# A sparse-attention kernel: early loads moved into five groups that wait for GpSimd

## The chip, the cores and the metric

The kernel runs on one core of a Trainium2 chip. The core has TensorE (PE, matmuls, with PEld for its weight loads), VectorE (DVE), ScalarE (ACT), GpSimd (POOL) and SyncE (SP, which here only issues DMAs). All DMAs of the core run on the same 16 DMA engines. The metric is device time in microseconds (us) of one execution; lower is better. On three runs the kernel before took 883.36, 886.07 and 886.86 us.

## The reference

```python
def _attn_ref(q, k, v):                      # q, k, v: 4 x 8 x 576 x 64
    scores = scale * np.matmul(q, k.transpose(0, 1, 3, 2))
    # heads 0-3: mask_local, the last 32 positions; heads 4-7: mask_strided, every 32nd
    scores = np.where(masks[None], scores, -1000000000.0)
    scores = scores - np.max(scores, axis=-1, keepdims=True)
    attn = np.exp(scores)
    attn = attn / (np.sum(attn, axis=-1, keepdims=True) + 1e-09)
    return np.matmul(attn, v)

def reference(...):
    x = attn_out as 2304 tokens x 512
    x = (sigmoid(x @ w_gate) * (x @ w_val)) @ w_out        # 512 -> 1536 -> 512
    return softplus(x @ w_in) @ w_out2                     # 512 -> 2048 -> 512
```

All of it is in fp32; a weight reaches the chip as 64-bit words, which the kernel takes apart into a high and a low part.

## The kernel before

The program is written in a fixed order by hand; nothing reorders it, so each engine works through its own instructions in the order of the code. Attention comes first. It is cut into 16 **units**, numbered 0 to 15: one batch and one pair of heads each, and in every four units two local and two strided ones. A unit i goes through these steps: `bias` and `scores` (PE matmuls into `ps_s`; L1011, L1030), a maximum and a subtraction on DVE (L1048, L1049), `exponent` on ACT (L1056), `normalize` (a sum and a reciprocal on DVE, L1063 to L1066, and the multiplication on POOL, L1069, in two halves), `p_transposes` (PE, L1090, copied out by ACT), `values` (PE, L1107) and `outputs`. `first()` runs units 0 to 3 and the start of unit 4 (`TURN`) with little else to fill PE; `stage(u)` then runs units 5 on, with the matmuls of the first dense layer (`ps_g`, `ps_v`, `ps_y`) between its steps. From about 220 us on the program is dense layers alone.

**Loads.** SP issues one DMA after the other: `load(i)` brings q and k of unit i (L917, L918), `load_v(i)` its v in two DMAs (L931), and `load_next()` one **piece of words**, 128 x 512 words of 8 bytes (L104). q, k, v and the pieces have three buffers each. The pieces are taken apart ("decoded") by `decode_steps`: DVE reads the piece first at L122 and last at L139, then ACT and POOL write the weights; its argument `refill` says whether it asks for another piece at its end. In `first()` the pieces 0, 1 and 2 are decoded (`decs[0]` to `decs[2]`), in `stage(5)` piece 3. Because engines are in order, DVE's L122 for piece 3 stands between unit 5's L1049 and L1063, and a late piece 3 holds up unit 5.

SP can have eight DMAs under way: each one uses one of eight semaphores in turn and waits for the DMA that had it before.

Of the kernel before, what the change touches and what calls it, by code (L numbers as in the profile page):

```python
# [9 lines left out]
F32 = mybir.dt.float32  # L10
# [38 lines left out]
def tile_sparse_attention_moe_moe2(  # L49
# [10 lines left out]
    nc = tc.nc  # L60
# [35 lines left out]
    raws = {}  # L96
    queue, todo = [], []

    def load_next():
        if todo:  # L100
            g, m, c = piece = todo.pop(0)
            src = w1[g, m] if g < NG1 else w2[g - NG1, m // 2]
            raw = rawp.tile([P, PIECE], U64, tag="raw", name="raw")
            nc.sync.dma_start(out=raw, in_=src[:, c * PIECE:(c + 1) * PIECE])  # L104
            raws[piece] = raw
            queue.append(piece)
# [37 lines left out]
    def decode_steps(pools, refill=True):  # L144
        (g, m, c), low, high, f, e = fields(pools)
        hi, lo = (x[:, c * PIECE:(c + 1) * PIECE] for x in wset[g % 2][m])
        high_part(pools, high, f)
        yield
        ff, ef = f.bitcast(F32), e.bitcast(F32)
        nc.scalar.activation(out=hi, in_=ff, func=AF.Copy)  # L150
        low_part(pools, low, f, e)
        pools["e"].tensor_tensor(out=ff, in0=ff, in1=hi.bitcast(F32), op=ALU.subtract)
        nc.gpsimd.tensor_tensor(out=lo, in0=ff, in1=ef, op=ALU.add)  # L153
        if refill:
            load_next()
        yield
# [75 lines left out]
    held = []  # L232
# [635 lines left out]
    def attention():  # L868
        with ExitStack() as actx:
# [16 lines left out]
            pools = {  # L886
                "g": pool("gp", 1), "t": pool("tp", 2), "d": pool("decp", 1), "e": nc.gpsimd,
                "hy": pool("ps_hy", 3, space=PSUM), "x": pool("ps_x", 1, space=PSUM),
            }
# [18 lines left out]
            def start_of(loc, r, i):  # L908
                return (r * NL[0] + i) * LQ if loc else (r * RH + i * RG) * NJ

            def load(i):
                b, hp = units[i]
                loc, w, m, ns = dims(i)
                qn, kn = (S, S + STRIDE) if loc else (QPAD, QPAD - HP + SQ)
                qq = qp.tile([P, QPAD], F32, tag="q", name="qt")
                kk = kp.tile([P, QPAD], F32, tag="k", name="kt")
                nc.sync.dma_start(out=qq[:, 0:qn], in_=q[b, hp][:, 0:qn])  # L917
                (nc.scalar if i < 2 else nc.sync).dma_start(  # L918
                    out=kk[:, 0:kn], in_=k[b, hp][:, 0:kn]
                )  # L920
                qt[i], kt[i] = qq, kk

            def load_v(i):
                b, hp = units[i]
                loc, w, m, ns = dims(i)
                t = vp.tile([P, NL[0], 2, D], F32, tag="v", name="vt")
                src = vl[b, hp] if loc else vs[b, hp - NLP]
                for r in range(HR):
                    n = NL[r] if loc else NS
                    o = r * HP  # L930
                    nc.sync.dma_start(out=t[o:o + w, 0:n], in_=src[r * w:(r + 1) * w, 0:n])  # L931
                vt[i] = t
# [7 lines left out]
            load_v(0)  # L940
            load_next()
            load(2)
            load_v(1)

            scratch = acc[NBA - 1]
            ident = scratch[:, 0:P]
# [216 lines left out]

            def first():

                decs = [decode_steps(pools, refill) for refill in (False, True, True)]
                bias(0)
                scores(0)
                masks[False] = table("m_str", P + 2 * LK, SQ, SLOTS_S, strided)
                exponent(0)  # L1170
                keep_busy(1)
                normalize(0)
                bias(1)
                scores(1)
                load_v(2)
                load(3)
                load_next()
                next(decs[0])
                exponent(1)
                keep_busy(2)  # L1180
                p_transposes(0)
                normalize(1)
                next(decs[0])
                bias(2)
                scores(2)
                values(0)
                load(4)
                load_v(3)
                load_next()
                outputs(0)  # L1190
                exponent(2)
                normalize(2)
                p_transposes(1)
                bias(3)
                scores(3)
                values(1)
                load_v(4)
                load(5)
                load_next()
                outputs(1)  # L1200
                exponent(3)
                normalize(3)
                next(decs[1])
                keep_busy(1)
                p_transposes(2)
                values(2)
                load_v(5)
                load(6)
                outputs(2)
                p_transposes(3)  # L1210
                next(decs[1])
                values(TURN - 1)
                outputs(TURN - 1)
                bias(TURN)
                scores(TURN)
                exponent(TURN)
                normalize(TURN)
                next(decs[2])
                yield
                next(decs[2])  # L1220
                yield
# [95 lines left out]
            for u in range(START, NU + SKEW):  # L1317
                t, pos = divmod(u - START, NPAIR)
# [172 lines left out]
```

## Time and profile before

| | us |
|---|---|
| runs of the kernel before | 883.36, 886.07, 886.86 (median 886.07) |
| the profiled execution | 887.23 |
| its span, from first to last instruction | 885.4 |
| PE busy (matmul records) | 865.7 |
| DVE / POOL / ACT busy | 598.2 / 490.2 / 420.6 |

The profiled execution took 1.16 us more than the median. The span is read by stretches: a wait at the start counts in full if nothing later takes it up, since PE is the engine that ends the program. "issue" behind an idle time means that the engine waited for nothing that the profile shows. PEclk is the granted clock of PE, 1.00 for 2.4 GHz and 0.50 for 1.2 GHz.

### The profile page before, as it was taken

To read this page: it belongs to the slowest core of one execution; us is meant where nothing else is said; L and a number is where in the kernel's file an instruction comes from. 1 tells how busy PE (TensorE), PEld (TensorE's weight loads), DVE (VectorE), ACT (ScalarE), POOL (GpSimd) and SP (SyncE) were. 2 spreads that over 40 slices of the span, in tenths; PEclk is the share of its full clock that TensorE was granted. 3 is DMA by queue.
4 is the path that set the end of the run, shared out by engine and by line. 5 is a ranking of instruction groups with operands and counts; after the bars stand their busy time and mean duration, and the time that the engine had idled before them with its cause. 6 is when DMAs were issued, how large, how long until landed. Compare 5 with 4: busy or idle time off the path is not lost.

```text
span 885.4 us, 15378 instructions
## 1 busy us (share of the span) xinstructions
PE 865.7 (98%) x6010; PEld 725.0 (82%) x6010; DVE 598.2 (68%) x898; ACT 420.6 (48%) x680; POOL 490.2 (55%) x389
## 2 busy tenths in 40 slices
PE   7799999999999999999999999999999999999998
PEld 5578878888888888888888888888888878888887
DVE  6696776268878888878874645665756574656574
ACT  2366544423333333233333466666667575665641
POOL 5373321037888687788778625466536963343630
PEclk9699999999999999999999999999999999999999
DMA  9696460034675577566644245566575565545403
GB/s 276 179 247 163 122 161 4 1 105 134 241 257 191 190 254 233 180 214 231 223 164 165 72 145 181 192 198 196 195 233 183 192 219 183 187 148 182 151 1 118
DMA packets 61367, 153.01 MB, mean 173 GB/s; under 512 B 6160, under 2 KB 6672, under 8 KB 61296
## 3 DMA queue, kind: packets, MB, share of 16 engines
q1 hardware_dynamic: 61008, 151.42, 53.3%
q8 instruction: 47, 0.77, 0.4%
q10 hardware_dynamic: 288, 0.62, 0.2%
q14 instruction: 24, 0.20, 0.1%
HBM read 113.75 MB, written 38.27 MB: 172 GB/s over the span
## 4 chain that ended last, share of the span: by engine, by line
PE 68%; DVE 4%; ACT 3%; POOL 3%; issue 1%; DVEq 0%; POOLq 0%; ACTq 0%
PE ps_y L72 9%; PE ps_y L73 9%; PE ps_y L74 9%; PE ps_v L72 4%; PE ps_v L74 4%; PE ps_v L73 4%; PE ps_g L72 4%; PE ps_g L74 4%; PE ps_g L73 4%; PE ps_h L74 3%; PE ps_h L73 3%; PE ps_h L72 3%; PE ps_b L72 2%; PE ps_b L73 2%; PE ps_b L74 2%
## 5 line engine op out<-in xcount | busy, mean ns | idle before, releaser
L330 POOL TENSOR_TENSOR b<-b,b 128x512 f32<-128x512 f32 (+1 forms) x42 | 72.5, 1739 | 91.7 <-DVE gl L330 46.1
L241 ACT ACTIVATE gh<-ps_v 128x512 fp32r<-128x512 f32 (+1 forms) x60 | 33.3, 555 | 131.5 <-DVE ps_v L284 131.5
L304 DVE TENSOR_TENSOR acc<-ps_y,acc 128x512 f32<-128x512 f32 (+1 forms) x100 | 62.2, 634 | 48.0 <-PE ps_y L74 47.6
L333 ACT ACTIVATE gh<-b 128x1024 fp32r<-128x1024 f32 (+1 forms) x63 | 57.8, 917 | 40.7 <-DVE b L713 23.9
L469 DVE TENSOR_TENSOR acc<-ps_y,acc 128x512 f32<-128x512 f32 x66 | 44.8, 686 | 41.7 <-PE ps_y L74 40.7
L330 POOL TENSOR_TENSOR gl<-b,gh 128x1024 fp32r<-128x1024 f32 x20 | 49.2, 2458 | 36.5 <-ACT gh L333 36.5
L242 DVE TENSOR_TENSOR gl<-ps_v,gh 128x512 fp32r<-128x512 f32 (+1 forms) x60 | 38.3, 638 | 37.5 <-ACT gh L241 37.5
L189 POOL TENSOR_TENSOR a<-f,e 128x512 f32<-128x512 f32 x32 | 41.4, 1295 | 39.6 <-DVE e L139 39.6
L177 POOL TENSOR_TENSOR pair<-a,pair 128x512 fp32r<-128x512 f32 x32 | 41.5, 1298 | 31.7 <-ACT pair L176 31.7
L330 DVE TENSOR_TENSOR gl<-b,gh 128x1024 fp32r<-128x1024 f32 (+1 forms) x43 | 48.7, 1134 | 14.5 <-ACT gh L333 14.3
L74 PE MATMUL ps_y<-gh,w02l 128*128 128x512 f32 (+1 forms) x144 | 53.8, 374 | 0.4 <-POOL w02l L153 0.4
L72 PE MATMUL ps_y<-gh,w12h 128*128 128x512 f32 (+1 forms) x144 | 54.1, 376 | 0.1
L73 PE MATMUL ps_y<-gl,w12h 128*128 128x512 f32 (+1 forms) x144 | 53.7, 373 | 0.0
L126 DVE SCALAR_TENSOR_TENSOR f<-raw,ps_x 128x512 uint32<-128x512 uint32 x68 | 46.8, 688 | 9.4 <-POOL w11l L153 2.1
L284 DVE TENSOR_TENSOR ps_v<-ps_v,sg 128x512 f32<-128x512 f32 (+1 forms) x60 | 38.5, 641 | 21.2 <-PE ps_v L74 20.0
L74 PE MATMUL ps_y<-gh,w12l 128*128 128x512 f32 (+1 forms) x140 | 52.2, 373 | 0.2 <-POOL w12l L153 0.2
L72 PE MATMUL ps_y<-gh,w02h 128*128 128x512 f32 (+1 forms) x136 | 51.3, 377 | 0.7 <-ACT acc L302 0.6
L176 ACT ACTIVATE pair<-s 128x512 fp32r<-128x512 f32 x32 | 20.2, 632 | 66.4 <-POOL s L203 51.8
L73 PE MATMUL ps_y<-gl,w02h 128*128 128x512 f32 (+1 forms) x136 | 50.7, 373 | 0.2 <-DVE gl L242 0.2
L139 DVE SCALAR_TENSOR_TENSOR e<-raw,ps_x 128x512 f32<-128x512 uint32 x68 | 46.7, 687 | 2.3
L132 DVE TENSOR_SCALAR ps_x<-f 128x512 uint32<-128x512 uint32 x68 | 46.8, 688 | 0.9
L122 DVE TENSOR_SCALAR ps_x<-raw 128x512 uint32<-128x512 uint32 x68 | 46.6, 685 | 0.0
(340 smaller groups left out, 2803.8 us busy)
## 6 DMA issues: line engine op xcount, KB each, us to landing
raw<-in_w_dram SPq DMA_DIRECT2D x68, 512.0 KB, 4.5
in_s<-pair SPq DMA_DIRECT2D x32, 512.0 KB, 2.9
out_s<-pair SPq DMA_DIRECT2D x32, 512.0 KB, 2.9
xh<-in_s SPq DMA_DIRECT2D x64, 256.0 KB, 2.9
xl<-in_s SPq DMA_DIRECT2D x56, 256.0 KB, 3.7
out_dram<-acc SPq DMA_DIRECT2D x16, 256.0 KB, 3.3
w10h<-out_s SPq DMA_DIRECT2D x6, 512.0 KB
w10l<-out_s SPq DMA_DIRECT2D x6, 512.0 KB, 4.0
```

The source lines that it names most:

```text
L72: nc.tensor.matmul(ps, lhsT=lh, rhs=rh, start=first, stop=False, **kw)
L73: nc.tensor.matmul(ps, lhsT=lh, rhs=rl, start=False, stop=False, **kw)
L74: nc.tensor.matmul(ps, lhsT=ll, rhs=rh, start=False, stop=last, **kw)
L122: nc.vector.tensor_scalar(out=part, in0=high, scalar1=3, scalar2=0x3FFFFFFF, op0=ALU.logical_shift_left, op1=ALU.bitwise_and,)
L126: nc.vector.scalar_tensor_tensor(out=f, in0=high, scalar=0xC0000000, in1=part, op0=ALU.bitwise_and, op1=ALU.bitwise_or,)
L132: nc.vector.tensor_scalar(out=e, in0=f, scalar1=0xFF800000, scalar2=None, op0=ALU.bitwise_and)
L139: nc.vector.scalar_tensor_tensor(out=e.bitcast(F32), in0=low, scalar=2.0 ** -52, in1=x.bitcast(F32), op0=ALU.mult, op1=ALU.mult,)
L177: nc.gpsimd.tensor_tensor(out=l, in0=src, in1=h.bitcast(F32), op=ALU.subtract)
L304: nc.vector.tensor_tensor(out=y, in0=ps[:, 0:n], in1=y, op=ALU.add)
L330: eng.tensor_tensor(out=out, in0=a, in1=b, op=ALU.subtract)
L333: nc.scalar.activation(out=op[0], in_=src, func=AF.Copy)
L469: nc.vector.tensor_tensor(out=y, in0=ps, in1=y, op=ALU.add)
```

## The change

A new helper `hold(t)` writes one element of a tile on GpSimd. Where a load is `held`, that write comes just before the load's DMA into the same tile, so the DMA has to wait for it; and as GpSimd works in order, the write comes only after what stands before it on GpSimd, which here is a unit's `normalize`. Since SP is in order too, everything behind a held DMA waits with it. v of units 1 to 5 is loaded like this, each with one or two other loads behind it: five groups. The second decoder of `first()` asks for no piece any more; the pieces are all asked for in `first()` itself.

```diff
+    def hold(t):
+        nc.gpsimd.memset(t[0:1, 0:1], 0.0)
...
-            def load_v(i):
+            def load_v(i, held=False):
...
+                if held:
+                    hold(t[:, 0, 0, :])
                 for r in range(HR):
...
             load(2)
-            load_v(1)
...
-                decs = [decode_steps(pools, refill) for refill in (False, True, True)]
+                decs = [decode_steps(pools, refill) for refill in (False, False, True)]
...
                 scores(1)
-                load_v(2)
                 load(3)
+                load_v(1, held=True)
                 load_next()
...
                 normalize(1)
+                load_v(2, held=True)
+                load(4)
...
                 values(0)
-                load(4)
-                load_v(3)
-                load_next()
                 outputs(0)
                 exponent(2)
                 normalize(2)
+                load_v(3, held=True)
+                load_next()
...
                 values(1)
-                load_v(4)
-                load(5)
-                load_next()
                 outputs(1)
                 exponent(3)
                 normalize(3)
+                load_v(4, held=True)
+                load(5)
...
                 values(2)
-                load_v(5)
-                load(6)
                 outputs(2)
...
                 normalize(TURN)
+                load_v(5, held=True)
+                load_next()
+                load(6)
+                load_next()
                 next(decs[2])
```

On SP, behind unit 2's k, stood in the kernel before (vt is v, raw a piece of words, qt and kt are q and k; the forms give the unit: vl and 576 or 608 columns are local units):

```order
L918 DMA kt_154<-in_k_dram 128x612
L931 DMA vt_157<-in_vl_dram 64x1280
L931 DMA vt_157<-in_vl_dram 64x1024
L931 DMA vt_337<-in_vs_dram 54x768 x2
L917 DMA qt_340<-in_q_dram 128x622
L918 DMA kt_341<-in_k_dram 128x612
L104 DMA raw_344<-in_w1_dram 128x512
```

The same place now:

```order
L925 DMA kt_154<-in_k_dram 128x612
L924 DMA qt_334<-in_q_dram 128x622
L925 DMA kt_335<-in_k_dram 128x612
L940 DMA vt_338<-in_vl_dram 64x1280
L940 DMA vt_338<-in_vl_dram 64x1024
L109 DMA raw_342<-in_w1_dram 128x512
L940 DMA vt_369<-in_vs_dram 54x768 x2
```

q and k of unit 3 have moved ahead of v of units 1 and 2, and v of unit 1 and of unit 2 each wait for GpSimd.

The second place is SP from v of unit 4 to the sixth piece of words, before:

```order
L931 DMA vt_540<-in_vl_dram 64x1280
L931 DMA vt_540<-in_vl_dram 64x1024
L917 DMA qt_543<-in_q_dram 128x576
L918 DMA kt_544<-in_k_dram 128x608
L104 DMA raw_547<-in_w1_dram 128x512
L931 DMA vt_601<-in_vl_dram 64x1280
L931 DMA vt_601<-in_vl_dram 64x1024
L917 DMA qt_604<-in_q_dram 128x622
L918 DMA kt_605<-in_k_dram 128x612
L104 DMA raw_627<-in_w1_dram 128x512
L104 DMA raw_724<-in_w1_dram 128x512
```

And now:

```order
L940 DMA vt_552<-in_vl_dram 64x1280
L940 DMA vt_552<-in_vl_dram 64x1024
L924 DMA qt_556<-in_q_dram 128x576
L925 DMA kt_557<-in_k_dram 128x608
L940 DMA vt_701<-in_vl_dram 64x1280
L940 DMA vt_701<-in_vl_dram 64x1024
L109 DMA raw_705<-in_w1_dram 128x512
L924 DMA qt_707<-in_q_dram 128x622
L925 DMA kt_708<-in_k_dram 128x612
L109 DMA raw_711<-in_w1_dram 128x512
L109 DMA raw_729<-in_w1_dram 128x512
```

The fourth piece of words (piece 3, counted from 0; now raw_705) has moved behind v of unit 5 (vt_701), which waits for GpSimd; so have q and k of unit 6 and pieces 4 and 5.

On GpSimd the hold for v of unit 5 stands right behind unit 4's normalisation (sl0), in the changed kernel:

```order
L1077 TENSOR_TENSOR sl0_109<-sl0_109,st_692 128x320 [waits DVE_49,Activation_49]
L1077 TENSOR_TENSOR sl0_109<-sl0_109,st_692 128x320
L100 MEMSET vt_701 1x1 [waits DMAHW7_49,DMAHW6_49,PE_49]
L157 TENSOR_TENSOR f_713<-f_713,w01h_68 128x512 [waits DVE_49,Activation_49,Pool_49]
```

The one-element write is new; its neighbours stand as before. On DVE nothing moved, and the reader of piece 3 stands inside unit 5 (st_777, sl1_110):

```order
L1056 TENSOR_REDUCE st_777<-ps_s_734 128x2x5 [waits PE_49]
L1057 TENSOR_TENSOR sl1_110<-ps_s_734,st_777 128x640 [waits DVE_49]
L127 TENSOR_SCALAR ps_x_798<-raw_705 128x512 [waits DMAHW3_49]
L131 SCALAR_TENSOR_TENSOR f_796<-raw_705,ps_x_798 128x512 [waits DVE_49,Pool_49]
L1071 TENSOR_REDUCE st_777<-sl1_110 128x2x5 [waits Activation_49]
```

What moved here is only the DMA that the third row waits for.

## Rows read from the trace of the kernel before

**Rows 1.** The page: instructions of each engine; PE and its clock in 40 slices.

```profile
PE 865.7 (98%) x6010; PEld 725.0 (82%) x6010; DVE 598.2 (68%) x898; ACT 420.6 (48%) x680; POOL 490.2 (55%) x389
...
PE   7799999999999999999999999999999999999998
...
PEclk9699999999999999999999999999999999999999
```

**Rows 2.** Busy time by stretch of the first 50 us; columns in the first line.

```profile
core 0: us, PE busy (x) PEld busy (x) DVE busy (x) ACT busy (x) POOL busy (x), PEclk, DMA share, GB/s
10.00:15.00 5.00, 5.00 (x115) 3.77 (x116) 4.48 (x8) 1.64 (x5) 1.40 (x2) 1.00 1.04 274
...
25.00:28.50 3.50, 2.60 (x56) 1.78 (x56) 3.36 (x7) 2.03 (x5) 1.42 (x2) 0.99 0.87 235
28.50:32.20 3.70, 3.41 (x107) 2.76 (x107) 1.64 (x3) 1.41 (x3) 2.55 (x2) 0.50 1.02 294
32.20:36.20 4.00, 0.03 (x4) 0.01 (x3) 0.00 (x0) 0.00 (x0) 0.00 (x0) 0.50 0.99 240
36.20:42.20 6.00, 5.91 (x111) 4.32 (x111) 4.22 (x8) 0.82 (x2) 1.33 (x2) 0.51 0.24 94
...
45.00:50.00 5.00, 5.00 (x106) 4.19 (x99) 4.66 (x10) 2.46 (x6) 2.75 (x4) 1.00 0.97 252
```

**Rows 3.** Timeline of PE, three waits inside a run: start, us, instruction, idle before.

```profile
16.65 0.34 PE L1030 MATMUL ps_s<-kt,qt 64*64 64x54 f32 x8 [1.20 <-issue]
...
21.93 0.37 PE L1030 MATMUL ps_s<-kt,qt 64*64 64x54 f32 x9 [1.75 <-issue]
...
36.19 0.64 PE L1030 MATMUL ps_s<-kt,qt 64*32 64x64 f32 x21 [3.97 <-issue]
```

**Rows 4.** Matmuls between those waits, counted by stretch (columns as in rows 2).

```profile
16.60:21.90 5.30, 3.54 (x126) 2.99 (x126) 3.94 (x7) 2.03 (x5) 4.32 (x6) 1.00 0.98 344
21.90:36.15 14.25, 8.63 (x252) 6.78 (x252) 7.45 (x12) 4.96 (x10) 4.38 (x5) 0.73 0.90 240
```

**Rows 5.** Instruction packets: whole span, then from 13:14.5, 19:20.5, 33:34 (packets, MB, share).

```profile
q8 instruction: 47, 0.77, 0.4%
...
q8 instruction: 1, 0.02, 5.3%
...
q8 instruction: 1, 0.02, 4.5%
...
q8 instruction: 1, 0.02, 8.1%
```

**Rows 6.** Timeline of POOL and DVE: a memset, normalisations of units 2 and 4, unit 3's maximum.

```profile
0.24 0.10 POOL L1474 MEMSET const-float32-0.0<- 128x1 f32 x1 [0.24 <-issue]
...
20.90 1.42 POOL L1069 TENSOR_TENSOR ss<-ss,st 128x324 f32<-128x324 f32 x2 [0.91 <-DVE st L1066]
...
22.40 0.83 DVE L1048 TENSOR_REDUCE st<-ps_s 128x12 f32<-128x648 f32 x1 [1.64 <-PE ps_s L1030]
...
40.87 1.40 POOL L1069 TENSOR_TENSOR sl<-sl,st 128x320 f32<-128x320 f32 x2 [8.85 <-DVE st L1066]
```

**Rows 7.** Timeline, first readers: v of unit 3, piece 3, k of units 6 and 7.

```profile
28.20 0.29 PE L1107 MATMUL ps_o<-pt,vt 54*64 54x54 f32 x2
...
45.04 0.68 DVE L122 TENSOR_SCALAR ps_x<-raw 128x512 uint32<-128x512 uint32 x1
...
48.14 0.92 PE L1030 MATMUL ps_s<-kt,qt 64*64 64x54 f32 x48
...
55.16 0.92 PE L1030 MATMUL ps_s<-kt,qt 64*64 64x54 f32 x48
```

**Rows 8.** Timeline of SP: issues from 23 to 44 us.

```profile
23.47 1.52 SPq L931 DMA_DIRECT2D vt<-in_vl_dram  x2
...
29.62 14.26 SPq L104 DMA_DIRECT2D raw<-in_w_dram  x2
```

**Rows 9.** One piece of words, handed out at 43.56 us: from issue to landing.

```profile
DMA to landing us min/median/max: 4.5/4.5/4.5
```

More of the change, by code (lines that the diff above doesn't have):

```diff
@@ L97, in tile_sparse_attention_moe_moe2, with load_next @@
     queue, todo = [], []
-    def load_next():
+    def hold(t):
+        nc.gpsimd.memset(t[0:1, 0:1], 0.0)
+    def load_next(held=False):
         if todo:
@@ L103, in load_next @@
             raw = rawp.tile([P, PIECE], U64, tag="raw", name="raw")
+            if held:
+                hold(raw.bitcast(F32))
             nc.sync.dma_start(out=raw, in_=src[:, c * PIECE:(c + 1) * PIECE])
@@ L909, in start_of, with load @@
                 return (r * NL[0] + i) * LQ if loc else (r * RH + i * RG) * NJ
-            def load(i):
+            def load(i, held=False):
                 b, hp = units[i]
@@ L916, in load @@
                 kk = kp.tile([P, QPAD], F32, tag="k", name="kt")
+                if held:
+                    hold(qq)
                 nc.sync.dma_start(out=qq[:, 0:qn], in_=q[b, hp][:, 0:qn])
@@ L927, in load_v @@
                 src = vl[b, hp] if loc else vs[b, hp - NLP]
+                if held:
+                    hold(t[:, 0, 0, :])
                 for r in range(HR):
```

## The prediction, made before the changed kernel ran

> **What bounds the kernel now.** I read the page first. PE's digits are below 9 in the first two slices and the last alone, and its granted clock dips once, in the second slice [rows 1]. The change touches only the first 60 us, so the question is what one microsecond there is worth: with PE full from the third slice on, a shift of PE at 60 us that nothing takes back shifts the end by as much. The next view was the busy time by stretch. From 32.2 to 36.2 us all five engines stand still, while the DMA engines are 0.99 busy [rows 2]. The timeline of PE names the wait: 3.97 us in the middle of unit 4's `scores`, after 59 of 80 matmuls that wait for no semaphore, with "issue" as the cause. Two more of this kind lie before it, 1.20 us in unit 2 and 1.75 us in unit 3 [rows 3]. They sit at a regular place: 126 matmuls lie from the first to the second and 252, twice as many, from the second to the third [rows 4].
>
> What is regular in the number of instructions is their own supply. Queue q8 brought 47 packets of 16 KB in the span [rows 5], and PE has 6010 matmuls and as many weight loads [rows 1]: 12,020 instructions over 47 packets is 256 each, 128 matmuls, or 126 with the semaphore instructions between them. One packet each began at 13 to 14.5, 19 to 20.5 and 33 to 34 us [rows 5], some 2 to 3 us before PE went on. So I take the three waits for late instruction packets. What made them late: SP handed out 3.46 MB from 23.47 to 30.2 us (v, q, k and words of units 4 to 6 and pieces 3 and 4; sizes from the forms in the listings) [rows 8], at some 260 GB/s 13 us of work, and the DMA engines are full until 36.2 us and slack behind it [rows 2]. The third packet began inside that backlog.
>
> The Trainium skill has two rules here. "Runtime: NRT & Kernel Launch", section "Instruction fetch mechanics", says that a sequencer fetches blocks of 16 KiB, 256 instructions, while it runs the one before, and that the crossing is mostly hidden. The block size agrees with the count above; "mostly hidden" does not agree with 3.97 us, and the measurement decides.
>
> **What the change removes.** It hands the same bytes out in smaller portions.
>
> *First wait, 1.20 us.* I count 0. DVE shows no wait for unit 2's scores, and it is DVE that PE's next step waits for; only unit 3's maximum waits for PE [rows 6]. Bounds 0 to 1.20; since the DVE chain hides it, the row at 22.40 us is the nearest.
>
> *Second wait, 1.75 us.* DVE waits 1.64 us for it [rows 6], and that is what the chain of unit 3 can win. But v of unit 1 and piece 1, 1.11 MB, are now handed out from 13.1 us on, just ahead of this packet, and take 4 us. I take 1.2; bounds 0.9 and 1.64.
>
> *Third wait, 3.97 us.* When its packet is asked for, around 26 us, only unit 3's v and piece 2 (0.86 MB, 3.3 us) lie ahead, in place of a part of the 3.46 MB. I take 3.5; bounds 2.0 and 3.97.
>
> Together the end of unit 4's scores, now at 36.19 + 0.64 = 36.83 us [rows 3], comes **4.7 us earlier** (2.9 to 5.6). PE's clock is at 0.50 from 28.5 to 42.2 us [rows 2]; if the denser work keeps it at 1.00, up to 1.0 more, since of 3.4 busy us before the third wait some 2 are matmuls and transposes that would take half. I leave this out of the sum and in the bounds.
>
> **What it adds.** Five one-element writes on POOL, 0.10 us each by the nearest memset [rows 6], 0 to 0.5 in all: POOL waits 0.91 and 8.85 us for DVE before the normalisations of that group of rows, which hides them, and behind a write stands only work that waits for DVE or ACT. Without that cover 0.5. Each write also waits for the old reader of its v buffer; that reader is two units back on PE and done, 0.
>
> v of unit 3 is released by unit 2's normalisation, 20.90 + 1.42 = 22.3 us. Its cost from there: a piece lands 4.5 us after issue on an idle queue [rows 9], of which 0.524 MB at 260 GB/s are 2.0 us, so **2.5 us plus the bytes**. (260: 252 GB/s at a share of 0.97 [rows 2].) With 0.33 MB that is 3.8 us, 26.3 us; `values` of unit 3 starts at 28.20 [rows 7], now 1.2 earlier: 27.0. I take 0, bounds 0 and 0.5.
>
> *The fifth group decides.* v of unit 5 waits for unit 4's normalisation, and behind it on SP wait piece 3, q and k of unit 6, pieces 4 and 5 and then v, q, k of units 6 and 7. In the kernel before all but the last of these were handed out by 30.2 us [rows 8] and long landed. Let T be the end of unit 4's scores. The normalisation ends at 40.87 + 1.40 = 42.27 [rows 6], T + 5.4; the hold and SP add about 0.2, so the group starts at T + 5.6.
> - Piece 3 lies behind v: 0.59 + 0.52 = 1.11 MB, 4.3 us; with 2.5 it lands at T + 12.4. DVE reads it now at 45.04 [rows 7], T + 8.2. **4.2 us late.** DVE is in order, so unit 5's sum, its normalisation and PE's transposes stand behind this read.
> - k of unit 6: 1.75 MB, 6.7 + 2.5, lands at T + 14.8; PE wants it at 48.14 [rows 7], T + 11.3. 3.5 us late.
> - k of unit 7: 3.76 MB, 14.4 + 2.5, at T + 22.5; wanted at 55.16 [rows 7], T + 18.3. 4.2 us late.
>
> The three lie along one path and do not add up: once the chain is 4.2 us behind, the other two land in time. So **4.2 us** are given back. Lower bound 3.1: piece 3 issued 1.2 us after v and landing 4.5 us later as if alone, T + 11.3. Upper bound 5.5: at the 240 GB/s of the stretch of the third wait [rows 2], k of unit 7 lands at T + 23.8.
>
> **Sum.** -4.7 + 4.2 = -0.5 us. On the profiled execution 887.23 - 0.5 = 886.7; that execution lies 1.16 us above the median, so on the median **885.6 us**. The ends: gain 5.6 (6.6 with the clock) against 3.1 is -2.5 (-3.5), gain 2.9 against 5.5 is +2.6. So 882.6 to 888.7 for the forecast alone.
>
> **Rivals.**
> *The gain stays.* If piece 3 and unit 6's q and k land before they are wanted, nothing is given back: 886.1 - 4.7 = 881.4. For it: the DMA engines do 274 GB/s at times and stand nearly idle before the group starts (0.24) [rows 2]. Against it: even alone, a piece takes 4.5 us and starts 6.8 us after T, and DVE wants it at T + 8.2.
>
> *The late packets come back, slower.* The fifth group puts 3.8 MB into the queue within some 7 us, more than the 3.46 MB that made the 3.97 us wait, and at least two of PE's instruction blocks come due between 47 and 62 us. Point of decision: a packet that begins less than some 2 us before PE reaches its block. Price: two waits like the second and the third, 1.75 + 3.97 = 5.7, on top of the forecast: 891.3. Against it: at a share of 0.97 from 45 to 50 us [rows 2] PE has no such wait today, and PE will mostly be standing for units 6 and 7 at the same time, which hides a part.
>
> *The holds don't help the packets.* If a packet does not queue behind the data, the three waits have another cause and stay; T stays, and only the give-back is left: 886.1 + 4.2 = 890.3. For it: none of the rows shows when a packet was asked for. Against it: the longest wait ends with the backlog, at 36.2 us [rows 2]. This is also what a rule of the Trainium skill would make of it: "DMA: Bandwidth & Descriptors", section "Queues, rings and completion order", says that each DMA engine goes round robin between its queue rows, packet by packet. By that rule a packet of q8 passes most of q1's backlog. The trace speaks against it so far as the packet at 33 us came 7 us after the place where I think it was asked for.
>
> **Chances.** Forecast 0.63, gain stays 0.15, packets come back 0.12, holds don't help 0.10. About 0.5%, 4.4 us, is what a measurement of this kernel can tell from no change: below 881.6 is faster, above 890.5 slower. Faster: most of the first rival, 0.14. Slower: most of the second and a part of the third, 0.13. Same 0.73. The range takes in the forecast, the upper half of the first rival and most of the third: 881.2 to 890.6, with about 2 in 10 left outside.
>
> **What would show it.** In the changed kernel's profile: no wait of over 0.5 us on "issue" inside unit 4's scores, whose end lies near 32 us; v of unit 5 issued some 5.6 us behind it; a DVE idle time of about 4 us before the decoder's first read of piece 3, put down to no engine or to a DMA; PE standing 2 to 3 us before unit 6's scores; from 62 us on the order of events as before, at nearly the same time. Wrong would be: scores of unit 4 ending at 35 us or later (the holds don't help), piece 3 read without a wait (the gain stays), or new "issue" waits between 47 and 62 us (packets come back).

## The result, and the profile after

The changed kernel takes **889.88 us** in the median (887.02 to 894.05), the kernel before 885.76 us in the same comparison (883.07 to 886.86): ratio 1.0053, 95% interval 1.0034 to 1.0071. It is slower by 4.1 us; the forecast was 885.6, no change. The profiled execution of the changed kernel spans 889.6 us, 4.2 more than that of the kernel before, so the two traces differ by about as much as the medians do. All lines stand 5 to 10 further down in the file (scores L1038, transposes L1098, normalisation L1077).

The two waits of [rows 3] that the forecast entered as a gain became shorter; the first did not occur in this trace. The timeline of PE in the changed kernel (start, us, instruction, idle before it and its cause):

```profile
20.54 0.38 PE L1038 MATMUL ps_s<-kt,qt 64*64 64x54 f32 x9 [0.34 <-issue]
...
32.12 0.64 PE L1038 MATMUL ps_s<-kt,qt 64*32 64x64 f32 x21 [2.44 <-issue]
...
47.16 0.92 PE L1038 MATMUL ps_s<-kt,qt 64*64 64x54 f32 x48 [3.04 <-DMA kt<-in_k_dram]
49.08 1.80 PE L1098 MATMUL ps_p<-one,sl 128*128 128x128 f32 x6 [0.99 <-POOL sl L1077]
...
59.59 0.92 PE L1038 MATMUL ps_s<-kt,qt 64*64 64x54 f32 x48
...
66.50 0.63 PE L1038 MATMUL ps_s<-kt,qt 64*32 64x64 f32 x37 [0.47 <-issue]
```

T, the end of unit 4's scores, is 32.12 + 0.64 = 32.76 us against 36.83: 4.07 gained. Then PE stands for k of unit 6 and for unit 5's normalisation, 4.0 us together. These transposes begin at 49.08, in the kernel before at 48.99: the whole gain is spent, as forecast. From there the forecast saw nothing more. Yet the scores of unit 7 begin at 59.59 and not at 55.16 [rows 7]: another 4.3 us went between the two marks, and the timeline lists no idle time of PE between them. The view by stretch tells where (columns in its first line):

```profile
core 0: us, PE busy (x) PEld busy (x) DVE busy (x) ACT busy (x) POOL busy (x), PEclk, DMA share, GB/s
...
32.20:36.20 4.00, 4.00 (x38) 2.92 (x46) 2.47 (x3) 0.74 (x1) 0.00 (x0) 0.50 0.04 14
44.00:48.00 4.00, 0.96 (x49) 0.82 (x48) 2.34 (x5) 0.63 (x1) 0.00 (x0) 1.00 0.98 341
48.00:52.00 4.00, 3.00 (x17) 2.24 (x11) 3.61 (x6) 1.03 (x2) 3.62 (x4) 0.55 1.04 283
52.00:56.00 4.00, 4.00 (x77) 3.19 (x76) 1.67 (x3) 1.84 (x3) 3.23 (x5) 0.50 1.00 293
56.00:60.00 4.00, 4.00 (x39) 3.09 (x40) 2.64 (x5) 3.24 (x6) 1.83 (x2) 0.67 0.47 155
```

PE is busy 0.96 of 4 us from 44 to 48; then its granted clock is at the lower of its two levels, 1.2 GHz, until some 58 us. From 49.1 us on it is "busy" all the time, and does about half the work: the same 48.0 to 58.4 us hold 217 matmuls in the kernel before (clock 1.00) and 98 here (0.52, with 1.0 us idle). On the page, 22 us to a slice, this is the 7 in the third place of the line of clocks, where [rows 1] has a 9; the second place has an 8 for a 6, since the clock was down there for a shorter time:

```profile
PEclk9879999999999999999999999999999999999999
```

The release of the fifth group went by the forecast's working. Timeline of POOL, SP and DVE in the changed kernel:

```profile
36.78 1.40 POOL L1077 TENSOR_TENSOR sl<-sl,st 128x320 f32<-128x320 f32 x2 [6.15 <-DVE st L1074]
38.12 0.09 POOL L100 MEMSET vt<- 1x1 f32 x1
...
38.23 1.11 SPq L940 DMA_DIRECT2D vt<-in_vl_dram  x2
...
45.48 0.69 DVE L127 TENSOR_SCALAR ps_x<-raw 128x512 uint32<-128x512 uint32 x1 [4.42 <-DMA raw<-in_w_dram]
```

The normalisation ends at T + 5.4, the hold takes 0.09 us, v of unit 5 is handed out at T + 5.5, and DVE reads piece 3 at T + 12.7 after 4.42 us of waiting (forecast: T + 5.6, T + 12.4, "about 4 us").

### The profile page after: what moved, and what is told of

Its sections match the earlier page's. It is cut to its first block, busy times and chain, and to the rows that moved or that the text cites. A ratio compares the mean times of both kernels' runs of the same rounds, so it can differ in the third digit from the quotient of the medians.

```text
span 889.6 us, 15388 instructions
## 1 busy us (share of the span) xinstructions
PE 868.9 (98%) x6010; PEld 727.1 (82%) x6010; DVE 598.4 (67%) x898; ACT 420.8 (47%) x680; POOL 490.2 (55%) x394
## 4 chain that ended last, share of the span: by engine, by line
PE 68%; DVE 4%; ACT 3%; POOL 3%; issue 1%; DMA 0%; DVEq 0%; ACTq 0%; POOLq 0%; SPq 0%
PE ps_y L72 9%; PE ps_y L73 9%; PE ps_y L74 9%; PE ps_v L72 4%; PE ps_v L74 4%; PE ps_v L73 4%; PE ps_g L72 4%; PE ps_g L74 4%; PE ps_g L73 4%; PE ps_h L74 3%; PE ps_h L73 3%; PE ps_h L72 3%; PE ps_b L72 2%; PE ps_b L73 2%; PE ps_b L74 2%
## 5 line engine op out<-in xcount | busy, mean ns | idle before, releaser
L335 POOL TENSOR_TENSOR gl<-b,gh 128x1024 fp32r<-128x1024 f32 x20 | 49.1, 2454 | 36.5 <-ACT gh L338 36.5
L335 DVE TENSOR_TENSOR gl<-b,gh 128x1024 fp32r<-128x1024 f32 (+1 forms) x43 | 48.7, 1134 | 14.5 <-ACT gh L338 14.3
L131 DVE SCALAR_TENSOR_TENSOR f<-raw,ps_x 128x512 uint32<-128x512 uint32 x68 | 46.8, 688 | 9.6 <-POOL w11l L158 2.1
L137 DVE TENSOR_SCALAR ps_x<-f 128x512 uint32<-128x512 uint32 x68 | 46.8, 688 | 0.9
```

The lines of the kernel that those rows point to most:

```text
L131: nc.vector.scalar_tensor_tensor(out=f, in0=high, scalar=0xC0000000, in1=part, op0=ALU.bitwise_and, op1=ALU.bitwise_or,)
L137: nc.vector.tensor_scalar(out=e, in0=f, scalar1=0xFF800000, scalar2=None, op0=ALU.bitwise_and)
L335: eng.tensor_tensor(out=out, in0=a, in1=b, op=ALU.subtract)
```

## The experiments

Theory A, formed on this: the first four groups win some 4 us; the fifth group gives that back by late data; and because PE stands for the data, its clock falls and costs some 4 us more. Rivals: the clock falls with the load on the DMA engines; instruction packets are late; handing out in bursts costs by itself. Times below are medians; every ratio is to the kernel before in the same comparison, whose own median lay between 885.2 and 886.2, so that times from different comparisons can be set against each other to some 0.5 us.

**1. Fill the time in which PE stands.** `keep_busy(n)` issues n matmuls of 128x512 whose output nobody reads.

```
                     bias(u)
+                    if u == 6:
+                        keep_busy(12)
                     scores(u)
+                    if u == 6:
+                        keep_busy(4)
```

> The changed kernel plus 16 matmuls of the kernel's own filler kind (128x512, no output used): 12 between unit 6's bias and scores, where PE stands 3.04 us for k of unit 6 (44.12 to 47.16), and 4 behind the scores, where it stands 1.00 us for unit 5's normalisation (48.08 to 49.08). The data come as late as before. Theory A (PE's standing is what makes its clock fall to 0.50 from 48.1 to 58.2 us, and that costs 4.3 us on top of the late data): the granted clock stays at 1.00 through 44 to 60 us, unit 7's scores start near 55.2 instead of 59.59, time 885.5 (889.9 - 4.3). Theory B (the clock falls with the load on the DMA engines, which are full from 43 to 56 us): the clock falls all the same, 889 to 890.

887.43 us, ratio 1.0017 (1.0005 to 1.0030): 2.45 us won by adding 16 matmuls of work. In its trace the clock stays up, while the DMA engines are as full as before, so it is not their load that lowers it:

```profile
44.00:48.00 4.00, 3.90 (x64) 2.95 (x56) 3.86 (x8) 1.12 (x3) 3.25 (x4) 1.00 1.03 315
48.00:52.00 4.00, 4.00 (x84) 3.23 (x83) 3.26 (x8) 3.95 (x8) 3.64 (x6) 1.00 0.96 306
```

This one execution ran at 1.00 throughout, so it proves less than the runs together. Each timed run lists its span and mean granted clock, and (1 - clock) x span x 2 is its time at half speed: 18.7 us in the median of the changed kernel's runs, 9.7 here, 10.6 in the kernel before (14.1 in each of the three later comparisons). Nine us at half speed are 4.5 us of work; 2.45 came back. Most of the rest can be found in waits that the slow clock had covered:

```profile
52.65 1.00 PE L1038 MATMUL ps_s<-kt,qt 64*64 64x54 f32 x48 [0.62 <-DMA kt<-in_k_dram]
...
59.24 0.44 PE L1038 MATMUL ps_s<-kt,qt 64*32 64x64 f32 x27 [0.66 <-DMA kt<-in_k_dram]
60.57 0.76 PE L1038 MATMUL ps_s<-kt,qt 64*32 64x64 f32 x53 [0.89 <-issue]
```

The Trainium skill, "TensorE: Matmul & The Clock Gate", section "HAM oscillation — how this bites in real kernels", says that waits for DMA which leave PE idle bring its clock down, and prices them at half of the time spent at the lower level. Here the half is 4.5 us and the kernel got 2.45 back, with waits of 1.28 us for late data and 0.89 on issue in the rows above.

**2. The same fillers in the kernel before.** The 16 matmuls also move everything behind them in PE's program; this run is the control.

> The kernel before with the same 16 filler matmuls that the filled version of the changed kernel has (12 between unit 6's bias and scores, 4 behind the scores). Here PE does not stand at this place and its clock is 1.00, so there is nothing to fill. Theory A (in the changed kernel the fillers help by keeping the clock up, and lie in time in which PE stands): here they cost their own time, 16 x 0.235 = 3.8 us, 889.5. Theory B (the 16 matmuls help there because they move the borders of PE's instruction blocks): they move them here too, and the time falls by some 2 us, or at least rises by less than 2 us.

888.94 us, ratio 1.0043 (1.0022 to 1.0063), 2.7 us more. That is less than 3.8, but a loss, and the interval (2.0 to 5.6 us) takes in theory A's 3.8 and not theory B's fall: the same fillers cost time where PE does not stand. The run showed something else. Up to 44 us its program is that of the kernel before, yet unit 4's scores run through without any wait:

```profile
31.30 1.41 PE L1030 MATMUL ps_s<-kt,qt 64*32 64x64 f32 x80
...
43.94 2.89 PE L965 MATMUL ps_w<-w12l,one 128*128 128x512 f32 x12
```

T is 32.71 here, the wait of 3.97 us [rows 3] is absent. It belongs to some executions of the kernel before, not to all.

**3. The fifth group handed out early**, behind the second half of piece 1's decoding and without a hold; groups one to four as in the change.

```
                 next(decs[1])
+                load_v(5)
+                load_next()
+                load(6)
+                load_next()
                 values(TURN - 1)
...
                 normalize(TURN)
-                load_v(5, held=True)
-                load_next()
-                load(6)
-                load_next()
```

> The changed kernel with its fifth group alone undone: v of unit 5, piece 3, q and k of unit 6 and piece 4 are handed out without a hold, behind the second half of piece 1's decoding, as soon as SP comes to them (near 28.5 us). Groups one to four keep their holds. Theory A (the fifth group's lateness costs 4.2 us of standing and 4.3 us of clock, and the first four groups keep their gain of 4.1): unit 4's scores end near 32.8, piece 3 is read without a wait, no wait over 0.3 us before unit 6's scores, clock 1.00 from 40 us on, time 881.4. Theory B (the bytes of the fifth group, handed out by 31 us, delay the instruction packet behind unit 4's scores again): that wait grows from 2.44 to some 4 us, unit 4's scores end at 34.5, time 883 to 885.

**882.69 us**, ratio 0.9971 (0.9955 to 0.9987): 7.2 us better than the change, 3.0 better than the kernel before. Theory A holds, with a smaller gain than 4.1. T is 33.53 in its trace, nothing is late for data, and PE waits for instructions in three new places:

```profile
47.11 0.76 PE L1098 MATMUL ps_p<-one,sl 128*128 128x128 f32 x5 [1.10 <-issue]
54.38 0.45 PE L1038 MATMUL ps_s<-kt,qt 64*64 64x54 f32 x15 [0.63 <-issue]
61.48 0.63 PE L1038 MATMUL ps_s<-kt,qt 64*32 64x64 f32 x37 [1.12 <-issue]
```

**4. The new order without the holds** (so five times), and **5. the fifth group alone** (in the kernel before).

```
-                load_v(1, held=True)
+                load_v(1)
```

In run 5 the second decoder of `first()` asks for no piece either, as in the change:

```
                 load(5)
-                load_next()
...
-                load_v(5)
-                load(6)
...
                 normalize(TURN)
+                load_v(5, held=True)
+                load_next()
+                load(6)
+                load_next()
```

> The changed kernel with the five holding writes left out: the loads stand in the new order, and SP hands each out as soon as its buffer is free. Theory A (what makes the packets of PE's instructions late is the amount of data outstanding): waits on issue of about 1.5 us in unit 3's and 4 us in unit 4's scores again, no late piece 3, time 885 to 887. Theory B (the order of the loads, not the waiting, moved the packets): the waits stay at 0.35 and 2.44 us, unit 4's scores end at 32.8, and since nothing is late behind that, 881 to 882.

> The kernel before with the fifth group alone: v of unit 5 is held until unit 4's normalisation, and behind it stand piece 3, q and k of unit 6, piece 4; the loads ahead of it stand as before, without holds. Theory A: the late data cost 4.2 us of standing plus 4.3 us of clock relative to the end of unit 4's scores; that end itself comes earlier if the 1.75 MB of the group were a part of the backlog behind which the third packet waits. So 894.3 if unit 4's scores end at 36.8 as before, 889 to 891 if they end near 33. Theory B (the group costs nothing by itself, the loss of the change comes from the first four groups): 886.

The order alone: 885.33 us, 0.9997 (0.9981 to 1.0014), nothing; a packet is late again (3.39 us, in unit 3's scores this time), as theory A had it. So the holds make the gain, 2.6 us by the two medians of 3 and 4; their intervals just touch, so its size is less sure than its sign. The fifth group alone: 889.12 us, 1.0043 (1.0028 to 1.0058), nearly as slow as the whole change, with the same stand (`scores` of unit 6) and 0.50 of clock behind it:

```profile
47.58 1.54 PE L1035 MATMUL ps_s<-kt,qt 64*64 64x54 f32 x48 [3.45 <-DMA kt<-in_k_dram]
```

**6. v of unit 5 behind q and k of unit 6.** Piece 3 takes the hold.

```
-                load_v(5, held=True)
-                load_next()
+                load_next(held=True)
                 load(6)
+                load_v(5)
                 load_next()
```

> The changed kernel with its fifth group in another order: the hold sits on piece 3, and v of unit 5 stands behind q and k of unit 6 (piece 3, q6, k6, v5, piece 4). Released at the same moment, by unit 4's normalisation. With T the end of unit 4's scores and 2.5 us plus the bytes at 260 GB/s, piece 3 lands at T + 10.1 (1.9 late instead of 4.2) and k of unit 6 at T + 12.6 (1.3 late instead of 3.5), while k of unit 7 has the same bytes ahead of it and lands at T + 22.5 as before (4.2 late). Theory A (the bytes of the whole burst set the lateness, and the clock falls where PE stands long in one piece): the give-back by data stays at 4 to 5 us, but it is split into shorter waits, the clock falls for a shorter time or not at all, 887.4 to 888.5. Theory B (piece 3's lateness alone is the give-back): 2.3 us less of it and the clock besides, 885.0 to 885.5.

888.30 us, 1.0026 (1.0008 to 1.0044): 1.6 us under the changed kernel by the medians, with intervals that overlap, where theory B had 4.5 to 5. Piece 3 now comes sooner (VectorE waits 2.11 us for it and not 4.42), but PE still stands 2.77 us for k of unit 6, the clock falls for a shorter time (14.2 us at half speed), and k of unit 8 is late as well:

```profile
47.98 1.16 PE L1038 MATMUL ps_s<-kt,qt 64*64 64x54 f32 x48 [2.77 <-DMA kt<-in_k_dram]
...
63.43 1.04 PE L1038 MATMUL ps_s<-kt,qt 64*32 64x64 f32 x80 [1.04 <-DMA kt<-in_k_dram]
```

So the order within the burst is worth 1.6 us at most by the medians; the burst as a whole stays late.

**7. The fifth group released 3.6 us earlier**, by a DVE write behind unit 4's subtraction, and **8. the same in the kernel before, fifth group alone.**

```
+    def hold(t, engine=None):
+        (engine or nc.gpsimd).memset(t[0:1, 0:1], 0.0)
...
+                    hold(t[:, 0, 0, :], nc.vector if i == 5 else None)
...
                 scores(TURN)
+                load_v(5, held=True)
+                load_next()
+                load(6)
+                load_next()
                 exponent(TURN)
                 normalize(TURN)
-                load_v(5, held=True)
-                load_next()
-                load(6)
-                load_next()
```

The cut shows run 7.

> The changed kernel with its fifth group released earlier: the holding write on v of unit 5 is made by VectorE behind unit 4's subtraction (T + 1.75 us in the changed kernel's trace) instead of GpSimd behind unit 4's normalisation (T + 5.4). All five groups stand as in the change otherwise. Theory A (the moment of the release sets the loss): the group starts 3.7 us sooner, piece 3 lands at T + 8.7 and k of unit 7 at T + 18.8, each some 0.5 late, PE does not stand long and its clock stays at 1.00 behind 40 us: 883.2 (882.5 to 884.5). Theory B (the loss comes from handing the group out in one burst, whenever that is): 888 to 890.

> The kernel before with the fifth group alone (v of unit 5, piece 3, q and k of unit 6, piece 4), released by VectorE behind unit 4's subtraction; the first four groups stand as before, without holds. Theory A (what the change can win comes from taking the fifth group's bytes out of the backlog of 23 to 30 us, and the first four groups add nothing): the same as with all five groups, 883.2. Theory B (the gain comes from the first four groups' holds): only the small lateness is left against the kernel before, 886.

884.10 us, 0.9978 (0.9965 to 0.9992), and 885.31 us, 0.9991 (0.9974 to 1.0009). The moment of release sets the loss: of the 7.2 us between the changed kernel and run 3 some 6 are back. The lateness was 2 us and not 0.5, but the clock did not fall:

```profile
41.35 0.69 DVE L127 TENSOR_SCALAR ps_x<-raw 128x512 uint32<-128x512 uint32 x1 [1.61 <-DMA raw<-in_w_dram]
...
44.77 0.92 PE L1038 MATMUL ps_s<-kt,qt 64*64 64x54 f32 x48 [1.96 <-DMA kt<-in_k_dram]
```

Run 8 lies between its two theories; 1.2 us separate it from run 7 and the intervals overlap, so what groups one to four add there is not settled by this pair.

**9. Only v of unit 5 and piece 4 held**, the rest as in run 7.

```
                 load(5)
+                load_next()
+                load(6)
...
                 load_v(5, held=True)
                 load_next()
-                load(6)
-                load_next()
```

> The kernel with the fifth group released by VectorE (884.1 us), with a part of that group taken ahead: piece 3, q and k of unit 6 (1.16 MB) stand without a hold behind k of unit 5, and only v of unit 5 and piece 4 wait for unit 4's subtraction. Theory A (what is left of the loss there is the 1.61 us of VectorE and 1.96 us of PE waiting for piece 3 and k of unit 6): both waits go, and since the 1.16 MB are handed out behind the crossing into the block that holds unit 4's scores, that block is not delayed by them: 882.0 (881.2 to 883.2). Theory B (the 1.16 MB delay the instruction packets of the next blocks instead): new waits on issue of 1 to 2 us at matmul 725 or 851, 883.5 to 885.

**882.69 us**, 0.9975 (0.9957 to 0.9992). Both waits are gone, as theory A had it, and the scores of units 6 and 7 begin at T + 11.3 and T + 18.7 (T = 31.53), where the kernel before has them, at T + 11.3 and T + 18.3:

```profile
42.84 0.92 PE L1038 MATMUL ps_s<-kt,qt 64*64 64x54 f32 x48
50.27 0.92 PE L1038 MATMUL ps_s<-kt,qt 64*64 64x54 f32 x48
```

Runs 3 and 9 are below the kernel before by 0.3%, which is under what was called no change; their intervals, and that of run 7, lie below 1.

**10. Pieces 1 and 2 one group later**, in the kernel of run 3, to have less data ahead of the packets.

```
                 load_v(1, held=True)
-                load_next()
...
                 load_v(2, held=True)
+                load_next()
                 load(4)
...
                 load_v(3, held=True)
-                load_next()
...
                 load(5)
+                load_next()
```

> The kernel of the fifth group handed out early (882.7 us), with pieces 1 and 2 one group later: piece 1 behind v of unit 2 instead of v of unit 1, piece 2 behind k of unit 5 instead of v of unit 3. Piece 1 is first read near 25 us and piece 2 near 36.5, so both still land in time. Theory A (a packet of PE's instructions waits behind what was handed out shortly before it): 0.52 MB less lies ahead of the packet of unit 3's scores and of unit 4's, their waits shrink to under 0.5 us each, time 881 to 882. Theory B (the packets' delay does not depend on that): no change, 882.7.

886.67 us, 1.0011 (0.9994 to 1.0029): some 4 us *worse* than run 3. Both theories fell. The wait in unit 3's scores is gone, but three others came, and the one in unit 5's transposes, 1.10 us in run 3, is 2.42:

```profile
25.17 0.44 PE L1115 MATMUL ps_o<-pt,vt 54*64 54x54 f32 x11 [1.15 <-issue]
...
32.62 0.64 PE L1038 MATMUL ps_s<-kt,qt 64*32 64x64 f32 x21 [2.20 <-issue]
...
42.20 1.25 PE L1115 MATMUL ps_o<-pt,vt 64*64 64x32 f32 x67 [1.19 <-issue]
...
49.55 0.66 PE L1098 MATMUL ps_p<-one,sl 128*128 128x128 f32 x4 [2.42 <-issue]
```

Counted from 0 at the program's start these are matmuls 473, 599, 725 and 852, 126 apart and, within one, at the same count as the waits of [rows 3], which are matmuls 221, 347 and 599: 95 + 126 k. Between two crossings q8 as a rule brings one packet, which I take for the block that PE will want at the second (in the kernel before and in run 1 one packet began 0.8 and 1.0 us ahead of the first crossing). Six crossings into the block before matmul 599 (times in us; the bytes are those handed out by SP less those that q1 had moved):

```
kernel          crosses 473   outstanding   packet begins   reaches 599   goes on
before             26.21        1.39 MB         33.32          32.20       36.19
run 2              26.41        1.33 MB         28.50          32.38         -  
changed            24.96        0.57 MB         29.40          29.66       32.12
run 1              24.81        0.31 MB         25.52          29.49         -  
run 9              25.15        0.22 MB         25.90          31.21         -  
run 10             25.17        0.00 MB         30.25          30.40       32.62
```

In the three rows with a wait PE goes on 2.4 to 2.9 us after the packet began, and the wait is what this way exceeds the block's own run of 5 to 6 us. In run 10 nothing was outstanding at the crossing, but group four (1.7 MB) and v of unit 5 behind it were handed out from 25.25 us, 0.08 us later, and the packet came 5.1 us after the crossing. So it is not the amount alone. That a group which falls just on a crossing delays the packet is a guess from this one row; in run 10 PE came there at that moment, presumably because its earlier wait was gone. The changed kernel and run 1 have the same program up to 40 us, and one packet slipped in before group four and the other did not. The kernel before and run 2 have the same program too, with nearly the same bytes outstanding, and their packets began 7.1 and 2.1 us after the crossing. What exactly orders a packet among the data stays open.

**11. Borders moved by 63 matmuls**: 64 narrow matmuls at the program's start in place of one filler, in the kernel before and in that of run 3.

```
-            keep_busy(6)
+            keep_busy(5)
+            ps = bank(pools, "y", "ps_w")
+            for _ in range(64):
+                nc.tensor.matmul(ps[:, 0:64], lhsT=one, rhs=idle[:, 0:64], start=True, stop=True)
```

> The kernel before with 63 more matmuls at the very start (64 of 128x64 in place of one filler of 128x512, in the time in which PE waits for q of unit 0). Everything behind is the same and stands 63 matmuls later in PE's program. Theory A (PE waits at the borders of its blocks of instructions): waits on issue again lie at matmul 95 + 126 k counted from the start (221, 347, 473, 599, 725, 851), so 63 matmuls earlier in the code, and none lies behind the 40th, 38th and 59th matmul of the scores of units 2, 3 and 4. How long they are depends on how many matmuls of what size the block before holds, so the time may go either way, 883 to 888. Theory B (the waits belong to these scores, for data or buffers that the trace doesn't name): they stay behind the 40th, 38th and 59th matmul of those scores, 885.9.

> The kernel with the fifth group handed out early (882.7 us) with the same 63 matmuls at the start. Theory A: the waits of its trace at matmul 851 (1.10 us), 979 (0.63) and 1105 (1.12), each in a row of small matmuls of transposes and scores, move 63 matmuls earlier in the code, into rows of 128x512 matmuls or elsewhere, and change in length: 881 to 884.5. Theory B: they stay where they are in the code, 882.7.

896.23 us, 1.0113 (1.0088 to 1.0138), and 896.74 us, 1.0126 (1.0098 to 1.0154). The times say nothing on borders, and both lie outside what was expected: the 64 matmuls took 13.70 us instead of the few I had reckoned, and unit 0 began over 10 us late, with its data long there. The first of the two still answers the question of place:

```profile
4.25 13.70 PE L1317 MATMUL ps_w<-w12l,one 128*128 128x64 f32 x64
...
48.88 0.94 PE L1030 MATMUL ps_s<-kt,qt 64*32 64x64 f32 x46 [4.19 <-issue]
```

The wait sits behind 34 of unit 5's 80 matmuls, where no trace had one, and that is matmul 725 of the program again. The second has one wait of over 0.3 us on issue in its first 80 us, 0.42 at matmul 853, in `values`. The borders belong to the count, not to the code.

## Why the prediction failed, step by step

Two steps of the forecast failed. The gain was put too high, and the give-back left out what PE's fallen clock costs behind the stand.

The table sets the starts of three scores against T; "late" is against the kernel before (T + 11.3, T + 18.3, T + 24.1), the time at half clock is the median over the timed runs, all in us. T and the marks are of one execution each.

```
kernel            T      unit 6   unit 7   unit 8   at half clock    median
before          36.83      -        -        -       10.6-14.1       885.8
changed         32.76     3.1      8.5      8.5         18.7         889.9
1 fillers       29.75     2.7      4.6      5.4          9.7         887.4
5 fifth alone   32.72     3.6      6.2      6.2         16.9         889.1
6 v5 last       33.84     2.8      4.4      5.5         14.2         888.3
7 DVE release   31.43     2.0      2.1      2.1          8.8         884.1
9 split         31.53     0.0      0.4      0.4          8.0         882.7
3 early         33.53     0.0      1.2      2.1          7.0         882.7
```

The traces hold no clock reading ahead of 14.8 us in the kernel before and 5.4 us in run 1; a 1.00 in a row there, as in the first of [rows 2], is none. The 80 matmuls of unit 1's scores took 1.40 us in the kernel before and 1.41 in the changed one, as they do at 0.50, and 1.04 in run 1. By matmul 220 the changed kernel is 1.25 us behind run 1 (15.04 against 13.79), with the same program: so much of the difference in T comes from the start.

*The first wait (0)* can't be told apart: with the same program up to that place it was 0, 1.39, 0.55, 0, 0.18 and 1.39 us (changed, runs 1, 3, 6, 7, 9).

*The second and third (1.2 and 3.5) and T (4.7 earlier).* In the pair of traces 1.41 and 1.53 us went, and T moved by 4.07, inside the bounds. But both sizes were taken from one execution. The second wait, 1.75 and 1.94 us in two traces of the old program (before, run 2), was 0.34 in the changed kernel and 1.48, 1.46, 1.20, 0.65 and 1.47 in runs 1, 3, 6, 7 and 9, which have its program up to there. With the change's program up to 30 us, T was 32.76, 29.75, 33.84 and 31.43 (changed, runs 1, 6, 7), with a third wait of 2.44, 0, 0 and 0; with that of the kernel before it was 36.83 and 32.71, with 3.97 and 0. Nor does the wait alone make T: run 6 has none and the latest T of the four, since its clock was down and PE came to matmul 599 only at 33.52 us, with the packet begun at 27.68. Its row by stretch (PE alone, then PEclk, DMA share and GB/s):

```profile
24.00:28.00 4.00, 3.88 (x55) 0.50 0.66 196
```

What the groups win in the median is what runs 3 and 9 keep, 3.0 and 2.5 us (885.66 - 882.69, 885.19 - 882.69). **The gain was put 1.7 us too high.** The nearest reason that the traces give is that waits which come in some executions, or are covered in some by a lower clock, were entered as if they came in full in all; how often each comes was not measured.

*The holds (0)* were right: 0.09 us each, hidden.

*v of unit 3 (0)* was right: no wait of `values` for it.

*The fifth group's data (4.2).* The marks came as worked out: piece 3 at T + 12.7 (forecast 12.4), unit 6's scores at T + 14.4 (14.8), and with the clock held up in run 1 unit 7's at T + 22.9 (22.5). That the three lie along one path was right up to there; unit 8's scores began 5.4 late in run 1, the last 0.66 us of it waiting for their k, which the forecast left out by stopping at unit 7. One reading of [rows 8] was off: piece 5 and v, q and k behind it went out from 43.6 us on in the kernel before, not by 30.2, so k of unit 7 itself started only 0.34 us later in the changed kernel (45.48 against 45.14); it was the data ahead of it that had moved.

*The term that was missing.* The forecast said that PE would stand 2 to 3 us before unit 6's scores and then priced the standing at its own length. It had used the clock on the side of the gain ("if the denser work keeps it at 1.00, up to 1.0 more") and not on the side of the give-back, though [rows 2] show 6 us at 0.50 behind the stand that ended at 36.2 us (the clock had been down since 28.5, before it). In the trace it cost 4.34 us (0.09 behind at the transposes, 4.43 at unit 7's scores); of this the fillers won back 2.45 net.

So in the medians: -3.0 for the first four groups, +7.2 for the fifth (889.88 - 882.69), of which at least 2.45 are the clock's and, by subtraction, some 4.7 late data and what goes with them; +4.2 in sum, 4.1 measured. The parts hold in this order only: taken the other way round, the fifth group alone costs 3.5 (run 5), and the first four then add 0.7, about nothing, instead of winning 3.0. So their gain shows only where the fifth group isn't late; why, no run here settles. **The give-back was put 3.0 us too low.** That the time still lay inside the stated range was luck: the range reached to 890.6 for a rival that did not happen, and the time is outside the 882.6 to 888.7 of the forecast's own path. With the clock's 2.45 alone carried, which only run 1 showed, the forecast would have pointed at a loss: -4.7 + 4.2 + 2.45 = +2.0.

*The rivals.* "The gain stays" did not happen, and runs 3 and 9 show what it is worth: 3 us, not 4.7. "The late packets come back" had nearly the right time (891.3) by the wrong mechanism: between 47 and 62 us the changed kernel has no wait on issue of over 0.3 us. They did come back in runs 3 and 10, though not in run 9, where PE came to matmul 851 sooner still (43.8 us against 45.7 and 46.8). "The holds don't help the packets" is refuted by runs 3 and 4, the same order with and without the holds of groups one to four: 882.7 and 885.3.

The Trainium skill's "mostly hidden" for a block's crossing ("Runtime: NRT & Kernel Launch", section "Instruction fetch mechanics") holds here where the block before runs long: 8.2 us from matmul 599 to 725, a packet 3.9 us after the crossing, no wait in the changed kernel. It fails where a block of small matmuls runs 4.7 us and the packet begins 4.4 us after the crossing (2.44 us of waiting); in run 1, with 0.7 us, the same block had no wait.

## What to carry to other kernels

Price a stand of PE twice: its own length, and the stretch behind it in case the clock falls, whose cost [rows 2] or any earlier stretch at 0.50 lets one read (not each stand is followed by one, see run 7); filling the stand with idle matmuls is a cheap way to learn how much of a loss is the clock. A hold that spreads loads out is worth its release time: work out when the last byte of the group lands against its reader, and release only what isn't wanted soon (run 9). And a wait that depends on how a small transfer meets a burst differs from execution to execution, so its size is a chance times a length, not the length in one trace.

## What was not expected of the hardware

- After PE had been busy 0.96 of 4 us, its clock stayed at half for about 10 us, most of them full work (48 to 58 us), in the changed kernel and, shorter, in runs 5 and 6; after 1.96 us of standing in run 7 it did not fall.
- A packet of 16 KB of PE's instructions began 4.4 us after the crossing in one execution and 0.7 us in another of the same program up to there (changed, run 1), 7.1 and 2.1 us in the kernel before and run 2.
- 64 matmuls of 128x64 with a full 128x128 weight took 0.21 us each (run 11), where the five fillers of 128x512 just ahead of them took 0.50: an eighth of the columns, but over 0.4 of the time. PEld was busy 5.00 of 5 us there, so narrow matmuls with a weight load each are no short filler. The granted clock of that stretch is not on record.
